# A third attention batch on the TensorE-transposed path, a split first token group, and masking by matmul in a fused attention and SiLU-MLP kernel

## The chip, the cores and the metric

The kernel runs on one core of a Trainium2 chip. The metric is the device time of one execution in microseconds (us), as a median of several executions. A single-core program has no second die to compare with; runs are called fast unless they lie more than 1.5% above the fastest of their kernel, and only fast runs are compared. The time of an execution is about 1.7 us longer than the span of its profile (before: 341.09 against 339.4).

## The reference

Windowed attention over 8 batches, 8 heads, 576 positions and 64 features; heads 0 to 3 see a plain window of the last 32 positions, heads 4 to 7 a dilated one (every fourth of the last 128). The result, 4608 tokens of 512 features, goes through a two-layer MLP.

```python
scores = scale * np.matmul(q, k.transpose(0, 1, 3, 2))
mask_plain = (rel >= 0) & (rel < 32)
mask_dil   = (rel >= 0) & (rel < 32 * 4) & (rel % 4 == 0)
scores = np.where(masks, scores, -1e9)              # heads 0-3 plain, 4-7 dilated
attn = softmax(scores)                              # q, k, v: (8, 8, 576, 64) float32
x = (attn @ v).transpose(0, 2, 1, 3).reshape(4608, 512)
h = x @ w_in                                        # (512, 2048)
out = (h * sigmoid(h)) @ w_out                      # (2048, 512)
```

## The kernel before

The Python code does not only emit instructions, it plans them: a small simulator with assumed durations and assumed DMA arrival times decides in which order the steps are put into each engine's queue. The order is then fixed, and each engine works through its queue in that order. Every number below that looks like a time in the code is such an assumption.

q and k must be transposed before the scores. There are two ways in the kernel:

- **TensorE path** (batches 0 and 1, `PEB = 2`): q and k are loaded to SBUF as fp16 (`nat`), transposed by TensorE against an identity (`td`, `ta`, `tb`), and the attention result is transposed back by TensorE (`xp`, `xd`) into `xA`.
- **DMA path** (all other batches): a GpSimd DMA casts q and k to an fp16 scratch in DRAM (`kq_s`), DMA transposes on the SP queue bring them in (`nat<-kq_s`, `kqT<-kq_s`; four of them make a "turn"), and the attention result goes out to `x_s` and comes back by another DMA transpose (`xA<-x_s`, `xR<-x_s`).

The MLP runs in groups of 512 tokens. Layer 1 of a group needs x of all its tokens, so it needs one or two batches of attention.

```python
GT = 512;  NG = NT // GT            # 9 groups
PEB = 2;  GA = 3;  XR = 4           # batches on the TensorE path; groups in xA; buffers xR
# ... (cut)
issue_nat(0)                        # q, k of batch 0, all heads
# ... identity, band masks (cut)
issue_v(0)
# ... (cut)
for f0 in range(0, DFF, FC):        # w_in, 4 DMAs
    nc.gpsimd.dma_start(out=w_in16[:, :, f0 : f0 + FC], in_=wi[:, :, f0 : f0 + FC])
issue_nat(1)
for f0 in range(0, NFF, 4):         # w_out, 4 DMAs
    nc.gpsimd.dma_start(out=w_out16[:, f0 : f0 + 4], in_=wo[:, f0 : f0 + 4])
issue_v(1)
# ... (cut)
def turn_gen(b):
    issue_turn(b)                   # four DMA transposes on the SP queue
    yield "DMA", 12.5
    if b + 1 < B:
        count(("L", b + 1), loads_need(b + 1), lambda: start_loads(b + 1))

def loads_gen(b):
    # fences on the turn of batch b-1 and on x of batch b-2 (cut)
    issue_v(b)
    issue_cast(b)                   # q, k to the fp16 scratch
    yield "DMA", max(9.0, 52.0 - plan.now)
    v_in[b].done = plan.now
    yield "DMA", 4.5
    count(("T", b), 2, lambda: start_turn(b))
# ... in scores(): (cut)
nc.tensor.matmul(sp[i][:, w*n : w*(n+1)], lhs, rhs, start=True, stop=True)
nc.scalar.activation(p2, both[:, :, :n], AF.Exp, scale=scale)
nc.vector.tensor_tensor(p2, p2, mk, ALU.mult)        # the mask
# ... layer 1, one step of 16 per group: (cut)
for c in range(HP):
    nc.tensor.matmul(h, w_in16[:, c, f*P : (f+1)*P], x_g[:, c], start=(c == 0), stop=(c == HP-1))
nc.scalar.activation(th, h, AF.Tanh, scale=0.5)
nc.vector.scalar_tensor_tensor(gTs[g][:, f], th, 1.0, h, ALU.add, ALU.mult)
```

The softmax here doesn't subtract the row's maximum and nothing guards it: scores larger than these inputs give would overflow.

## Time and profile before

| | before |
|---|---|
| time, median | 337.68 us (337.23 to 342.65, 3 runs) |
| profiled run | 341.09 us, so 3.4 us above the median |
| first layer-1 matmul | 28.80 us |
| TensorE busy | 304.1 us of 339.4 |

The page of the kernel before. PE is TensorE, DVE is VectorE, ACT is ScalarE. The rows of digits give the busy tenths in 40 equal slices of the span (8.5 us each); PEclk is the clock granted to TensorE, in tenths.

```profile
span 339.4 us, 5670 instructions
...
PE 304.1 (90%) x2200; PEld 147.2 (43%) x2200; DVE 200.3 (59%) x477; ACT 154.2 (45%) x258; POOL 49.5 (15%) x78
...
PE   0678998999999883999999999599999999999995
...
PEclk9999999999999997999999999879999999999999
...
```

TensorE is close to full except at the start, in slices 14 to 16 and slice 26. The timeline of TensorE at the start of the kernel before (start, length, line, operation, output and inputs, shape, count, and in brackets the idle time before it and its releaser):

```profile
...
10.76 1.04 PE L404 MATMUL td<-ident,nat 96*128 96x96 f16 x11 [3.87 <-DMA nat<-in_q_dram]
...
28.80 4.93 PE L636 MATMUL h<-xA,w_in 128*128 128x512 f16 x12
34.10 2.07 PE L636 MATMUL h<-xA,w_in 128*128 128x512 f16 x8 [0.36 <-DVE gT L647]
...
```

The first transposes wait for data until 10.76 us; layer 1 begins at 28.80, and its first 12 matmuls take 4.93 us where eight take 2.07 later: the clock is still low. (The row PEclk shows 9 there all the same. The trace has no clock record before 32.93 us, and the page counts time without a record as full clock; in the first slices the matmul durations have to be read instead.) The waits of TensorE from 60 us on (total, times, longest):

```profile
...
PE h L636 <- DMA xR<-x_s: 6.0, 1, 6.0
PE s L434 <- DMA nat<-kq_s: 3.6, 1, 3.6
...
```

Two waits for DMA stand out: 6.0 us for the transposed x of batch 3 (it ends at 132.5 us) and 3.6 us for the transposed k and q of batch 7. The SP queue ahead of the first:

```profile
...
115.03 6.91 SPq L131 DMA_TRANSPOSE nat<-kq_s  x2
122.04 2.72 SPq L135 DMA_TRANSPOSE kqT<-kq_s  x2
124.85 0.85 SPq L507 DMA_DIRECT2D x_s<-oD  x1
127.77 2.53 SPq L326 DMA_TRANSPOSE xR<-x_s  x1
```

The last store of batch 3 (`x_s<-oD`) stands in the queue behind the turn of batch 4, and the transpose back to `xR` follows it.

### The profile page before, as it was taken

To read this page: it belongs to the slowest core of one execution; us is meant where nothing else is said; L and a number is where in the kernel's file an instruction comes from. 1 tells how busy PE (TensorE), PEld (TensorE's weight loads), DVE (VectorE), ACT (ScalarE), POOL (GpSimd) and SP (SyncE) were. 2 spreads that over 40 slices of the span, in tenths; PEclk is the share of its full clock that TensorE was granted. 3 is DMA by queue.
4 is the path that set the end of the run, shared out by engine and by line. 5 is a ranking of instruction groups with operands and counts; after the bars stand their busy time and mean duration, and the time that the engine had idled before them with its cause. 6 is when DMAs were issued, how large, how long until landed. Compare 5 with 4: busy or idle time off the path is not lost.

```text
span 339.4 us, 5670 instructions
## 1 busy us (share of the span) xinstructions
PE 304.1 (90%) x2200; PEld 147.2 (43%) x2200; DVE 200.3 (59%) x477; ACT 154.2 (45%) x258; POOL 49.5 (15%) x78
## 2 busy tenths in 40 slices
PE   0678998999999883999999999599999999999995
PEld 0553544444444331445444344244444444444442
DVE  5684779859977641698776368477654254145100
ACT  1464664156545440666455366254454344244211
POOL 8823410140005003100320050000000000000000
PEclk9999999999999997999999999879999999999999
DMA  8999999899759995995699989972260100200121
GB/s 104 187 206 199 204 174 214 180 165 214 163 150 147 205 214 80 192 231 143 150 188 228 212 106 202 221 138 77 79 144 33 62 31 0 95 1 31 64 93 62
DMA packets 115899, 47.42 MB, mean 140 GB/s; under 512 B 82592, under 2 KB 111264, under 8 KB 115872
## 3 DMA queue, kind: packets, MB, share of 16 engines
q0 software_dynamic: 47152, 19.92, 47.5%
q1 hardware_dynamic: 63536, 17.70, 26.6%
q10 hardware_dynamic: 5184, 9.44, 8.1%
q8 instruction: 17, 0.28, 0.3%
q14 instruction: 10, 0.08, 0.1%
HBM read 39.84 MB, written 20.05 MB: 176 GB/s over the span
## 4 chain that ended last, share of the span: by engine, by line
PE 80%; DVE 7%; DMA 6%; ACT 4%; issue 1%; POOL 1%; ACTq 0%; SPq 0%; POOLq 0%
PE y L664 36%; PE h L636 35%; PE s L434 3%; PE av_d L470 2%; DMA nat<-in_q_dram 2%; DVE gT L647 2%; PE av_p L470 2%; ACT th L645 2%; ACT ob L675 1%; DMA xR<-x_s 1%; DMA nat<-kq_s 1%; DVE oD L474 1%; DVE oP L474 1%; PE td L404 1%; DVE probs L449 1%
## 5 line engine op out<-in xcount | busy, mean ns | idle before, releaser
L647 DVE SCALAR_TENSOR_TENSOR gT<-th,h 128x512 f16<-128x512 f32 x144 | 98.0, 684 | 79.9 <-ACT th L645 79.7
L664 PE MATMUL y<-w_out,gT 128*128 128x512 f16 x576 | 140.3, 381 | 2.4 <-ACT ob L675 1.9
L645 ACT ACTIVATE th<-h 128x512 f32<-128x512 f32 x144 | 86.1, 598 | 93.3 <-PE h L636 89.0
L636 PE MATMUL h<-xR,w_in 128*128 128x512 f16 x384 | 95.7, 388 | 6.1 <-DMA xR<-x_s 6.0
L636 PEld LDWEIGHTS <-w_in 128*128 128x128 f16 x576 | 54.8, 100 | 73.7 <-issue 12.0
L664 PEld LDWEIGHTS <-gT 128*128 128x128 f16 x576 | 53.2, 98 | 60.8 <-issue 3.0
L636 PE MATMUL h<-xA,w_in 128*128 128x512 f16 x192 | 48.5, 390 | 2.8 <-DVE gT L647 2.6
L442 ACT ACTIVATE probs<-s 128x768 f16<-128x768 f32 (+2 forms) x45 | 36.4, 810 | 22.3 <-PE s L434 19.8
L675 ACT ACTIVATE ob<-y 128x512 f32<-128x512 f32 x36 | 21.5, 597 | 50.1 <-PE y L664 49.9
L470 PEld LDWEIGHTS <-probs 128*128 128x128 f16 x448 | 23.5, 102 | 15.5 <-issue 1.9
L474 DVE TENSOR_TENSOR oD<-av_d,rcps 72x256 f16<-72x256 f32 x64 | 26.9, 421 | 2.2
L474 DVE TENSOR_TENSOR oP<-av_p,rcps 96x256 f16<-96x256 f32 x48 | 20.2, 421 | 1.6
L449 DVE TENSOR_TENSOR probs<-probs,mask_d 128x864 f16<-128x864 f16 (+1 forms) x24 | 13.2, 552 | 6.8 <-ACT probs L442 6.6
L310 POOL COPY fence<-kqT 128x1 f16<-128x1 f16 x10 | 2.4, 240 | 99.7 <-DMA kqT<-kq_s 99.7
L470 PE MATMUL av_d<-vd,probs 128*128 128x65 f16 x256 | 15.9, 201 | 1.0 <-DVE rcps L473 0.6
L449 DVE TENSOR_TENSOR probs<-probs,mask_p 128x768 f16<-128x768 f16 x24 | 13.3, 553 | 6.0 <-ACT probs L442 5.7
L473 DVE RECIPROCAL rcps<-av_d 72x4 f32<-72x4 f32 x64 | 11.0, 172 | 7.6 <-PE av_d L470 7.5
L470 PE MATMUL av_p<-vp,probs 128*128 128x65 f16 x192 | 13.4, 200 | 1.5 <-DVE probs L449 0.9
L404 PE MATMUL td<-ident,nat 96*128 96x96 f16 x48 | 4.3, 242 | 10.5 <-DMA nat<-in_k_dram 6.6
L155 POOL DMA_DIRECT2D vp<-in_v_dram x8 | 11.6, 1446 | 3.5 <-PE td L404 1.9
L141 POOL DMA_DIRECT2D vraw<-in_v_dram x16 | 10.8, 677 | 5.1 <-DMA nat<-in_k_dram 2.4
L473 DVE RECIPROCAL rcps<-av_p 96x4 f32<-96x4 f32 x48 | 8.3, 174 | 4.3 <-PE av_p L470 3.6
(62 smaller groups left out, 117.0 us busy)
## 6 DMA issues: line engine op xcount, KB each, us to landing
out_dram<-ob ACTq DMA_DIRECT2D x36, 256.0 KB, 2.1
kq_s<-in_k_dram POOLq DMA_DIRECT2D x6, 576.0 KB, 9.8
kq_s<-in_q_dram POOLq DMA_DIRECT2D x6, 576.0 KB, 12.5
vp<-in_v_dram POOLq DMA_DIRECT2D x7, 384.0 KB, 7.5
w_in<-in_moe_w_in_dram POOLq DMA_DIRECT2D x4, 512.0 KB, 11.9
w_out<-in_moe_w_out_dram POOLq DMA_DIRECT2D x4, 512.0 KB, 16.6
vraw<-in_v_dram POOLq DMA_DIRECT2D x8, 224.0 KB, 5.6
x_s<-oP SPq DMA_DIRECT2D x12, 144.0 KB, 2.6
```

The lines of the kernel that those rows point to most:

```text
L141: nc.gpsimd.dma_start(out=vraw[p0 : p0 + m1 - m0, ab].rearrange("p h r d -> p h (r d)"), in_=src[m0:m1],)
L155: nc.gpsimd.dma_start(out=vp[:, j0:, :D], in_=win)
L442: nc.scalar.activation(p2, both[:, :, :n], AF.Exp, scale=scale)
L449: nc.vector.tensor_tensor(p2, p2, mk, ALU.mult)
L470: nc.tensor.matmul(a[:, i, : D + 1], lhs(i), rhs(i), start=True, stop=True)
L473: nc.vector.reciprocal(rcp[:n], a[:n, :, D : D + 1])
L474: nc.vector.tensor_tensor(o, a[:n, :, :D], rcp[:n, :, None].broadcast_to([n, HN, D]), ALU.mult)
L636: nc.tensor.matmul(h, w_in16[:, c, f * P : (f + 1) * P], x_g[:, c], start=(c == 0), stop=(c == HP - 1),)
L645: nc.scalar.activation(th, h, AF.Tanh, scale=0.5)
L647: nc.vector.scalar_tensor_tensor(gTs[g][:, f], th, 1.0, h, ALU.add, ALU.mult)
L664: nc.tensor.matmul(y, gTs[g][:, f, tb * P : (tb + 1) * P], w_out16[:, f], start=(f == 0), stop=(f == NFF - 1),)
L675: nc.scalar.activation(ob, y, AF.Copy, scale=0.5)
```

## The change

Its intent: TensorE waits for the DMA path, so one more batch is kept off it (`PEB = 3`), and the start is shortened: the dilated half of batch 0 is loaded and attended first; the first 512 tokens become two groups of 256, so that layer 1 can begin after half of batch 0; the masks of batch 0 are added in PSUM, where the results of matmuls collect, by a matmul (identity times 0 or -32768) instead of being multiplied on VectorE; layer 1 of the first two groups may use five PSUM buffers. Layer 2's weights are loaded before batch 1, and a turn is issued in four parts, so that stores can slip between its transposes.

```diff
-    NG = NT // GT
+    GROUPS = [(0, GT // 2), (GT // 2, GT // 2)] + [(t, GT) for t in range(GT, NT, GT)]
+    NG = len(GROUPS)
-    PEB = 2
-    GA = 3
-    XR = 4
+    PEB = 3
+    GA = 4
+    XR = 3
+    BIG = 32768.0
+    BIASED = (0,)
@@ start (cut) @@
-    issue_nat(0)
+    issue_nat(0, HN, H)              # dilated heads first
     make_identity(nc, ident)
-    issue_v(0)
+    issue_vraw(0)
+    issue_nat(0, 0, HN)              # then the plain heads
+    issue_vp(0)
+    nc.vector.tensor_scalar(band, band, 1.0, BIG, ALU.subtract, ALU.mult)
     # w_in
-    issue_nat(1)
     # w_out
-    issue_v(1)
+    issue_nat(1, 0, H)
+    issue_vraw(1)
+    issue_vp(1)
+    def third_batch():
+        issue_nat(2, 0, H)
+        issue_vraw(2)
+        issue_vp(2)
+        issue_cast(PEB)
+        yield "DMA", 0.0
@@ turns (cut) @@
-        issue_turn(b)
-        yield "DMA", 12.5
+        for n, us in enumerate((3.0, 3.0, 1.5, 7.5)):
+            issue_turn(b, n)
+            yield "DMA", us
@@ scores (cut) @@
+            if biased:
+                for i in range(2):
+                    nc.tensor.matmul(sp[i][:, : w * len(blocks)], ident, bs, start=True, stop=False)
@@
-                        sp[i][:, w * n : w * (n + 1)], lhs, rhs, start=True, stop=True
+                        sp[i][:, w * n : w * (n + 1)], lhs, rhs, start=not biased,
+                        stop=not biased or n == len(blocks) - 1,
@@
+            if biased:
+                return
             nc.vector.tensor_tensor(p2, p2, mk, ALU.mult)
@@ layer 1 (cut) @@
-            Step(lambda ring, f=f: l1(f), 0.87, ["h"], list(deps) + [AT_WIN[f // 4]], ("ACT", "DVE"))
+            Step(
+                lambda ring, f=f: l1(ring, f), 0.01 + w / 595, ["h", "x"] if g < 2 else ["h"],
+                list(deps) + [AT_WIN[f // 4]], ("ACT", "DVE"),
+            )
```

Cut from the diff: new orders of the attention steps, copies that go to whichever of ACT and DVE the planner finds free, seven score sets instead of six on the TensorE path, and new assumed arrival times.

## The prediction

> **What bounds the kernel now.** TensorE: busy 304 of 339.4 us (page, part 1), 80% of the chain that ended last. Adding each matmul at its warm interval (four 128x512 in 0.86 us in the timeline; small ones about 32 ns) gives an estimated 287 us of work. The other 52 us, by PE's timeline, the waits and the table of stretches:
> 1. Start: first matmul at 6.6 us, q of batch 0 lands at 10.6, layer 1 begins at 28.8 with 7.9 us of warm work done: 21 us lost. Batch 0's attention is one chain of short PE, ACT and DVE steps.
> 2. Layer 1 alone, 29 to 37: 1.2 us a step instead of 0.86, through two PSUM buffers, tanh (0.60) and multiply (0.69). With the cold clock, 4 us.
> 3. 126.5 to 132.5: layer 1 waits 6.0 us for batch 3's transposed x (xR<-x_s). In the SP queue batch 3's last store stands behind batch 4's transposes, which wait for a cast. Granted clock then 0.83 over 10 us: 8 us in all.
> 4. 214.8 to 218.4: scores of batch 7 wait 3.6 us for nat<-kq_s, then clock 0.86 and 0.80: 7 us.
> 5. 4 us after the last matmul; small waits.
> The Trainium skill, "TensorE: Matmul & The Clock Gate", Part 1, says an idle TensorE falls to half clock until busy about 3.4 us; the granted clock agrees (0.83 after the 6.0 us wait).
>
> **What the change does.**
> - PE gains 14 bias matmuls (4608 columns, 1.9 us warm, twice that cold) and a third batch's transposes (3.1): by the instruction orders 292 us, +5.3.
> - Start: dilated half of k and q first, so transposes start near 8.4 instead of 10.7; seven mask multiplies (0.45 to 0.6 us each, two in the chain) go. Layer 1 begins on 256 tokens after three of six plain blocks and half the dilated ones: first matmul at 21 to 23 with 8.0 done. Loss 14, gain 7.
> - Layer 1 of two half groups over five buffers: gain about 2.
> - Layer 2's weights before batch 1: layer 2 starts near 43, batch 1's data arrive then, and its attention (29 us long in the old timeline, 37 to 66) must fit beside 14 us of layer 2: 2 to 4 us of new waits around 45 to 65.
> - One batch fewer on the DMA path, its first cast early, its transposes split in four so stores slip between: the chain load, cast, transpose, attention, store, transpose leads TensorE by an estimated 15 us. Stalls 3 and 4 mostly go: gain 10 to 15.
>
> **Sum.** 339.4 + 5 - 7 - 2 + 3 - 13, some eaten by small waits of the planned in-order queue: 319 to 325 on the profile's scale, the timed median about 1 lower. I predict 321 us, 80% range 313 to 330. Faster by over 2%: 0.87; within 2%: 0.10; slower: 0.03.
>
> **What would show it.** First h matmul near 22 us (wrong after 25). No wait above 2 us on xR, xA<-x_s or nat<-kq_s after 100 us, clock 1.0 in every slice from there. PE waits of a few us on DVE and ACT between 45 and 65. No mask multiplies on DVE in batch 0; bias matmuls near 0.24 us cold.
>
> **What would make it wrong.** The DMA stalls stay or move (batch 4's cast waits for batch 2's readers); the PE order, fixed from assumed arrivals, meets later data (w_out near 28 to 36, batch 1 near 42), each miss idling PE and costing a warm-up; half-size matmuls hide weight loads less well (98 against 107 ns).

## The result, and the profile after

| | before | after |
|---|---|---|
| time, median | 337.88 us (337.23 to 342.65, 4 runs) | 328.11 us (327.89 to 328.73, 4 runs) |
| ratio of fast runs | | 0.972 (95%: 0.9697 to 0.9743) |
| span of the profile | 339.4 us | 327.0 us |
| first layer-1 matmul | 28.80 us | 24.93 us |

A ratio is the mean time of one kernel's fast runs over the mean of the other's fast runs of the same rounds, so it is not quite the ratio of the medians in the table. The change makes the kernel 2.8% faster; I had forecast 321 us, and it takes 328. The profiles differ by 12.4 us, the medians by 9.8, because the profiled run before was a slow one of its kind.

The page after:

```profile
span 327.0 us, 6033 instructions
...
PE 306.0 (94%) x2354; PEld 156.4 (48%) x2354; DVE 203.3 (62%) x501; ACT 160.8 (49%) x296; POOL 52.9 (16%) x83
...
PE   0798999898999999999999999899999999999995
...
PEclk9999999989999999999999999999999999999999
...
```

The low slices in the middle are gone. TensorE at the start of the changed kernel:

```profile
...
8.43 2.00 PE L465 MATMUL td<-ident,nat 96*128 96x96 f16 x23 [2.93 <-DMA nat<-in_q_dram]
...
15.44 0.50 PE L440 MATMUL ta<-ident,pair_rest 96*128 96x96 f16 x4 [0.79 <-DVE pair_rest L523]
...
24.93 0.60 PE L717 MATMUL h<-xA,w_in 128*128 128x256 f16 x4
...
29.24 3.23 PE L717 MATMUL h<-xA,w_in 128*128 128x256 f16 x28
...
44.92 0.93 PE L465 MATMUL td<-ident,nat 96*128 96x96 f16 x18
...
66.30 1.91 PE L717 MATMUL h<-xA,w_in 128*128 128x512 f16 x4
...
```

The dilated transposes start at 8.43, as forecast. The plain ones cannot finish before 15.44, and layer 1 begins at 24.93, two to four us later than forecast. Then 28 half-size matmuls take 3.23 us with their drain: the weight loads stay hidden behind the smaller matmuls. Batch 1 starts at 44.92, when its data land. At 66.30 four matmuls of the next group need 1.91 us instead of about 1.03: TensorE had been waiting on the end of batch 1's attention, and the clock had dropped (granted clock 0.83 between 60 and 70 us). The chain that ended last names what 15.44 waits for, the plain half of q:

```profile
...
5.42 1.31 POOL vraw L146 x2
6.72 1.88 POOL nat L116 x3
8.61 6.32 DMA nat<-in_q_dram
15.44 1.15 PE ta L440 x12
...
```

It lands at 14.93 us, behind v; before, all of batch 0 was in by 10.6. The waits of TensorE from 60 us on, and the SP queue around the first transpose back:

```profile
...
PE s L500 <- DMA nat<-kq_s: 1.2, 1, 1.2
...
```

```profile
...
100.99 2.85 SPq L137 DMA_TRANSPOSE nat<-kq_s  x1
...
115.18 0.84 SPq L580 DMA_DIRECT2D x_s<-oD  x1
117.98 1.38 SPq L369 DMA_TRANSPOSE xA<-x_s  x1
```

No DMA wait above 1.2 us is left. The turn of batch 4 starts at 100.99 us, against 115.03 before. x of the first batch on the DMA path is being transposed at 117.98 us, and TensorE reaches the group that needs it at 124.33.

**Where the time went.** To compare kernels whose queues are ordered differently, I use "lost time": the start of the first layer-1 matmul of a group, minus the estimated warm duration of all matmuls ahead of it in TensorE's queue. The durations are intervals read from the timelines: 0.216 us for 512 columns (four in 0.86), 0.110 for 256, 0.043 for 96, 0.033 for 65 or 72. The position in the trace is found by counting; the counts of trace and instruction list agree to within 4 records, so the values hold to about half a microsecond, but beside a wait a miscount of one matmul is worth the whole wait. Token 1536 of the kernel before and of b_turn4 is such a place, and there the first matmul that reads xR is taken from the trace:

```profile
...
132.49 3.28 PE L636 MATMUL h<-xR,w_in 128*128 128x512 f16 x8 [5.97 <-DMA xR<-x_s]
...
```

The sum of all work by the same estimate is 286.9 us before and 292.2 after.

| lost time (us) at the group that begins at token | 0 | 512 | 1024 | 1536 | 2048 | 3072 | 4096 |
|---|---|---|---|---|---|---|---|
| before | 21.8 | 28.3 | 30.2 | 38.8 | 40.7 | 48.3 | 48.0 |
| after | 17.0 | 21.9 | 26.7 | 27.1 | 27.8 | 30.5 | 30.9 |

After the last group only full-speed MLP work and a tail of 4 us follow. Up to token 512 the change gains 6.4 us; it gives back 2.9 of them by token 1024; from 1024 to the end it gains another 13.6; and it adds 5.3 us of work. That makes 11.8 of the 12.4 us. But a table of gains in order of time does not say which part of the change caused them: for that, parts were taken out.

### The profile page after: what moved, and what is told of

Read it like the earlier page. It is cut to its first block, busy times and chain, and to the rows that moved or that the text cites. A ratio compares the mean times of both kernels' runs of the same rounds, so it can differ in the third digit from the quotient of the medians.

```text
span 327.0 us, 6033 instructions
## 1 busy us (share of the span) xinstructions
PE 306.0 (94%) x2354; PEld 156.4 (48%) x2354; DVE 203.3 (62%) x501; ACT 160.8 (49%) x296; POOL 52.9 (16%) x83
## 4 chain that ended last, share of the span: by engine, by line
PE 80%; DVE 9%; DMA 4%; ACT 3%; POOL 2%; issue 1%; ACTq 0%; SPq 0%; POOLq 0%
PE y L750 36%; PE h L717 34%; PE s L500 3%; DVE gT L728 3%; DVE oD L549 2%; DMA nat<-in_q_dram 2%; DMA nat<-kq_s 2%; PE av_d L545 2%; PE av_p L545 2%; POOL nat L116 1%; DVE oP L549 1%; ACT ob L761 1%; DVE rcps L548 1%; PE td L465 1%; PE ta L440 1%
## 5 line engine op out<-in xcount | busy, mean ns | idle before, releaser
L750 PE MATMUL y<-w_out,gT 128*128 128x512 f16 x576 | 138.7, 379 | 0.9 <-ACT ob L761 0.9
L728 DVE SCALAR_TENSOR_TENSOR gT<-th,h 128x512 f16<-128x512 f32 (+1 forms) x160 | 99.6, 630 | 58.7 <-ACT th L726 57.7
L726 ACT ACTIVATE th<-h 128x512 f32<-128x512 f32 (+1 forms) x160 | 88.8, 556 | 77.4 <-PE h L717 71.0
L717 PEld LDWEIGHTS <-w_in 128*128 128x128 f16 x640 | 59.5, 98 | 55.2 <-issue 4.1
L717 PE MATMUL h<-xR,w_in 128*128 128x512 f16 x320 | 76.5, 379 | 0.5 <-DVE gT L728 0.4
L717 PE MATMUL h<-xA,w_in 128*128 128x512 f16 (+1 forms) x320 | 63.5, 339 | 1.3 <-DVE oD L549 0.7
L509 ACT ACTIVATE probs<-s 128x768 f16<-128x768 f32 (+2 forms) x45 | 35.0, 777 | 28.7 <-PE s L500 24.8
L761 ACT ACTIVATE ob<-y 128x512 f32<-128x512 f32 x36 | 21.5, 598 | 45.0 <-PE y L750 44.9
L545 PEld LDWEIGHTS <-probs 128*128 128x128 f16 x448 | 22.5, 99 | 12.6 <-DVE probs L518 0.4
L549 DVE TENSOR_TENSOR oD<-av_d,rcps 72x256 f16<-72x256 f32 x64 | 26.9, 421 | 2.2
L549 DVE TENSOR_TENSOR oP<-av_p,rcps 96x256 f16<-96x256 f32 x48 | 20.2, 421 | 1.6
L518 DVE TENSOR_TENSOR probs<-probs,mask_p 128x768 f16<-128x768 f16 x21 | 11.6, 554 | 8.8 <-ACT probs L509 8.8
L518 DVE TENSOR_TENSOR probs<-probs,mask_d 128x576 f16<-128x576 f16 (+1 forms) x23 | 11.9, 517 | 2.9 <-ACT probs L509 2.6
L465 PE MATMUL td<-ident,nat 96*128 96x96 f16 x72 | 5.7, 249 | 8.2 <-DMA nat<-in_k_dram 5.2
L163 POOL DMA_DIRECT2D vp<-in_v_dram x8 | 11.7, 1466 | 8.9 <-PE av_p L545 6.2
## 6 DMA issues: line engine op xcount, KB each, us to landing
w_in<-in_moe_w_in_dram POOLq DMA_DIRECT2D x4, 512.0 KB, 11.4
w_out<-in_moe_w_out_dram POOLq DMA_DIRECT2D x4, 512.0 KB, 17.9
```

The costliest lines, as they stand in the source:

```text
L163: nc.gpsimd.dma_start(out=vp[:, j0:, :D], in_=win)
L545: nc.tensor.matmul(a[:, i, : D + 1], lhs(i), rhs(i), start=True, stop=True)
L549: nc.vector.tensor_tensor(o, a[:n, :, :D], rcp[:n, :, None].broadcast_to([n, HN, D]), ALU.mult)
L717: nc.tensor.matmul(h[:, :w], w_in16[:, c, f * P : (f + 1) * P], x_g[:, c], start=(c == 0), stop=(c == HP - 1),)
L726: nc.scalar.activation(th[:, :w], h[:, :w], AF.Tanh, scale=0.5)
L728: nc.vector.scalar_tensor_tensor(gTs[g][:, f, :w], th[:, :w], 1.0, h[:, :w], ALU.add, ALU.mult)
```

## The experiments

Twelve kernels in three lots of four. The four of a lot ran on the same chip and share their runs of the kernel before, which took 338.69, 340.91 and 338.51 us (median) in the three lots; the lots are rows 1 to 4, 5 to 8 and 9 to 12 of the table. Neither times nor ratios compare freely across lots. In each lot the kernel before has executions below 339.1 us and others above 340. In the second lot five of those above 340 count as fast, in the other two none does, so the mean of its fast runs is 338.0, 340.3 and 336.9 us, and that alone makes the ratios of the second lot 0.7 to 1% lower than those of the others. The second and third lots ran on the same chip, so there a time can also be set beside that of the control after_again, 327.62 us. All gave a correct result.

| kernel | median us | ratio to before (95%) | first layer-1 matmul |
|---|---|---|---|
| a_nobias | 327.21 | 0.9685 (0.9659 to 0.9711) | 26.57 |
| a_nosplit | 327.06 | 0.9685 (0.9656 to 0.9715) | 29.20 |
| a_peb2 | 338.17 | 1.0018 (0.9982 to 1.0053) | 24.15 |
| b_turn4 | 337.05 | 0.9955 (0.9917 to 0.9993) | 29.07 |
| c_third | 330.20 | 0.9691 (0.9641 to 0.9740) | 28.59 |
| a_both | 328.83 | 0.9661 (0.9612 to 0.9710) | 30.20 |
| a_warm | 327.57 | 0.9615 (0.9567 to 0.9664) | 24.81 |
| a_b1first | 328.35 | 0.9629 (0.9572 to 0.9686) | 24.57 |
| after_again | 327.62 | 0.9736 (0.9694 to 0.9778) | 25.83 |
| a_peb2_cast1 | 370.00 | 1.0921 (1.0825 to 1.1017) | 25.23 |
| a_best | 321.63 | 0.9559 (0.9521 to 0.9597) | 24.57 |
| a_best2 | 373.04 | 1.1041 (1.0967 to 1.1116) | 21.07 |

The lost times:

| lost time (us) at token | 0 | 512 | 1024 | 1536 | 2048 | 3072 | 4096 |
|---|---|---|---|---|---|---|---|
| a_peb2 | 16.2 | 20.5 | 27.3 | 36.8 | 41.9 | 43.4 | 43.1 |
| b_turn4 | 21.2 | 29.5 | 32.4 | 42.3 | 45.2 | 47.3 | 47.1 |
| a_nosplit | 20.2 | 25.2 | 26.7 | 26.8 | 27.2 | 28.9 | 29.1 |
| c_third | 21.5 | 30.1 | 30.6 | 31.1 | 31.6 | 32.2 | 31.9 |
| a_both | 23.2 | 26.9 | 29.3 | 30.0 | 31.0 | 31.9 | 31.8 |
| a_b1first | 16.6 | 22.5 | 23.7 | 24.4 | 24.8 | 30.7 | 30.1 |
| a_best | 16.6 | 20.2 | 20.4 | 21.1 | 22.2 | 23.1 | 23.0 |

### a_nobias: masks multiplied again

```diff
-    BIASED = (0,)
+    BIASED = ()
-    nc.vector.tensor_scalar(band, band, 1.0, BIG, ALU.subtract, ALU.mult)
-    nc.vector.memset(mask_p[:W, :2], -BIG)
+    nc.vector.memset(mask_p[:W, :2], 0.0)
```

> The changed kernel with the bias matmuls of batch 0 taken out and the seven mask multiplies on DVE put back (everything else kept, the planner re-plans the order). Theory A (the start is limited by TensorE itself at the cold clock, and the 14 bias matmuls are 3 to 4 us of it between 10 and 24 us): first layer-1 matmul 2 to 3 us earlier than 24.9, time 325 to 327 us against 328.1. Rival (the reason for the change: two multiplies and their hops leave the chain): first layer-1 matmul about 1 us later, time 329 to 330.

Measured: first layer-1 matmul at 26.57 us, 1.6 us later than in the changed kernel, and 327.21 us, ratio 0.9685. Each theory got one half wrong. Theory A's early start did not come: TensorE loses the bias matmuls but waits for the multiplies instead. The rival's later start came, but not its longer time. The bias matmul does shorten the start, by 1.6 us against the changed kernel's profile and by 0.7 against the control's (25.83), and nothing of it reaches the end.

### a_nosplit: one first group of 512 tokens

```diff
-    GROUPS = [(0, GT // 2), (GT // 2, GT // 2)] + [(t, GT) for t in range(GT, NT, GT)]
+    GROUPS = [(t, GT) for t in range(0, NT, GT)]
```

> The changed kernel with the first 512 tokens as one group again. Theory A: layer 1 can then begin only after the whole of batch 0, first matmul 28 to 29 us instead of 24.9, though the attention before it no longer shares TensorE with layer 1: time 330 to 332 against 328.1. Rival (the chain to the end of batch 0 is what counts, and the early half only fills gaps that layer 2 or later steps would give back): within 1 us of 328.1.

Measured: the start was as theory A said, 29.20 us; the time was as the rival said, 327.06 us. In the table of lost times a_nosplit is 3.3 us behind the changed kernel at token 512 and level with it at token 1024 (26.7 both). Whatever layer 1 gains by beginning 4.3 us earlier is gone 30 us later.

### a_peb2: the third batch taken out

```diff
-    PEB = 3
-    GA = 4
-    XR = 3
+    PEB = 2
+    GA = 3
+    XR = 4
     def third_batch():
-        issue_nat(2, 0, H)
-        issue_vraw(2)
-        issue_vp(2)
         issue_cast(PEB)
```

(One more wait in the planner's list lets the first cast be issued before its turn, and the assumed arrival of that cast is 55 us instead of 64.)

> The changed kernel with two batches on the TensorE-transposed path again, the start and the four-part turns kept. Theory A (the third batch gives the DMA path its lead, and without it waits of 3 us or more on xR or nat<-kq_s come back after 90 us): time 331 to 335. Rival B (the four-part turns alone cured the DMA waits, and the third batch only adds 3.1 us of transposes to TensorE): 324 to 326 with no wait above 2 us.

Measured: 338.17 us, ratio 1.0018: all of the gain is gone, more than theory A had said. This kernel starts layer 1 at 24.15 us and is 7.8 us ahead of the kernel before at token 512 (20.5 lost against 28.3). Of that lead 2.9 us are left at token 1024 and 2.0 at token 1536 (36.8 against 38.8), and at token 2048 it is 1.2 us behind. Its waits from 60 us on:

```profile
...
PE h L715 <- DVE gT L726: 4.9, 9, 1.6
PE h L715 <- DMA xR<-x_s: 4.5, 1, 4.5
...
```

The wait for xR is back, and its transpose was issued at 128.26 us, against 127.77 before. The DMA path runs at its own pace (the turn of batch 4 starts at 117.4 us, against 115.0 before), and TensorE, arriving early, only waits more: first in layer-1 steps for VectorE, then for the DMA itself. That those steps wait because few layer-2 steps run beside them is my reading, not shown. (At token 4096 this profile has lost 4.9 us less than that of the kernel before, for 2.3 us more of work, and its span is 2.8 us shorter. The profiled run before was a slow one of its kind; the medians of the lot, 338.17 and 338.69, are the comparison.)

### b_turn4: the kernel before with the turn in four parts

```diff
-        issue_turn(b)
-        yield "DMA", 12.5
+        for n, us in enumerate((3.0, 3.0, 1.5, 7.5)):
+            issue_turn(b, n)
+            yield "DMA", us
```

> The kernel before with one edit: the four transposes of a turn are issued at four times of the plan, so the stores of the batch before slip between them in the SP queue. Theory B (the 6.0 us wait for x of batch 3 came from the order of the SP queue): that wait goes, time 330 to 333 against 337.9. Rival A (the chain of load, cast, transpose, attention, store is too long for its lead whatever the queue's order): the waits stay or move, 336 to 339.

Measured: 337.05 us, ratio 0.9955; the record's verdict is "unclear". Theory B falls: it was my reading of the SP queue in the prediction. Stores now do stand between the transposes, and the wait has moved:

```profile
...
PE h L637 <- DMA xR<-x_s: 3.6, 1, 3.6
...
```

```profile
...
122.40 3.10 SPq L132 DMA_TRANSPOSE nat<-kq_s  x1
...
136.05 2.20 SPq L327 DMA_TRANSPOSE xR<-x_s  x1
...
```

The turn of batch 4 is now at 122.40 instead of 115.03, and the transpose to xR at 136.05 instead of 127.77. Letting one transfer pass another did not shorten the chain. (This profile, of 340.2 us, and that of the kernel before are both of slower executions; of the faster ones there is no profile.)

### c_third: the third batch nearly alone

The edits of a_nobias and a_nosplit, and the loads as in the kernel before: batch 0 whole, batch 1's k and q before w_out. The new orders and the turns in four parts stay.

> The third batch nearly alone: the changed kernel with one first group of 512 tokens, mask multiplies instead of bias matmuls, batch 0 loaded whole and batch 1's k and q loaded before layer 2's weights, as in the kernel before. Theory C (the third batch is the whole gain; the early start is given back by 100 us): time 326 to 329 against 337.9 for before and about 328 for the changed kernel. Rival (the gain needs both, the start and the third batch): 331 to 334.

Measured: ratio 0.9691, with layer 1 starting at 28.59 as before the change; the median of 330.20 us goes with 340.91 for the kernel before in this lot. Theory C holds in the main. By the ratio the gain is whole without the early start; by the time it is 2.6 us short of the control on the same chip (330.20 against 327.62), which leaves 8.3 of the 10.9 us that the control gains on the kernel before in its lot. So the third batch carries three quarters of the gain or more. (c_third keeps the new orders and the four-part turns; whether the third batch needs them was not tested. Without the third batch, in a_peb2, they gain nothing.) The lost time at token 512 (30.1) is even larger than before (28.3), and from there to the end only 1.8 us are added, against 19.7 before.

What the third batch does can be read from the SP queues. The turn of batch 4 in c_third:

```profile
...
99.31 3.33 SPq L137 DMA_TRANSPOSE nat<-kq_s  x1
...
```

The turns of batches 3, 4, 5, 6 and 7 start at 79.0, 115.0, 145.5, 180.0 and 210.3 us before; at 65.3, 101.0, 135.1, 168.3 and 202.2 after; and at 61.7, 99.3, 129.7, 162.2 and 193.8 in c_third. Without the third batch, in a_peb2, they are at 82.8, 117.4, 148.5, 183.5 and 214.3. The first batch that goes through the scratch is then batch 3; its cast is issued at 49.7 us instead of 69.9, and the path keeps that lead of 8 to 18 us to the end.

### a_both: bias and split both undone

> The changed kernel with both the bias matmuls and the split of the first group undone. Alone each measured 0.9685 of before against 0.972 for the changed kernel. Theory C (neither matters to the end, each costs about 1 us of extra TensorE work): 325.5 to 327.5. Rival (one of the two is needed to keep the start short): 329 to 331.

Measured: ratio 0.9661, 328.83 us where before takes 340.91. By the ratio theory C holds again (0.9661 of 337.9 us is 326.4); by the time it lies between the two theories, 1.2 us above the control. The difference to c_third is only the order of the loads: a_both has lost less at token 512 (26.9 against 30.1) and loses 4.9 us from there to the end, where c_third, with batch 1 before layer 2's weights, loses 1.8.

### a_warm: dummy matmuls before the first data

```diff
+    nc.vector.memset(xA[:, 0, :512], 1.0)
+    hot = ps_s.tile([P, 2, 512], F32, tag="s", name="hot")
+    for _ in range(16):
+        nc.tensor.matmul(hot[:, 0], xA[:, 0, :P], xA[:, 0, :512], start=True, stop=True)
     issue_nat(0, HN, H)
```

> The changed kernel with 16 dummy matmuls of 512 columns on a constant tile before the data arrive, to have TensorE's clock granted before 8.4 us. The result is not touched. Theory C (batch 1's k and q land near 45 us, and its attention ends near 65 whatever the start does): first layer-1 matmul moves from 24.9 to 21 to 23 us, and the time stays within 1 us of 328. Rival A (the start counts in full): 324 to 326.

Measured: first layer-1 matmul at 24.81 us, not 21 to 23; 327.57 us. The dummies brought the clock up, and it was lost again. Stretches of 2 us (length, then busy us and instructions of each engine, granted clock, DMA share, GB/s):

```profile
...
8.00:10.00 2.00, 2.00 (x33) 1.43 (x31) 1.98 (x8) 0.00 (x0) 2.00 (x4) 1.00 1.15 144
10.00:12.00 2.00, 1.58 (x29) 0.92 (x25) 1.14 (x4) 1.23 (x3) 1.96 (x2) 1.00 1.17 147
12.00:14.00 2.00, 0.80 (x12) 0.49 (x9) 1.35 (x4) 0.06 (x1) 1.36 (x2) 0.79 1.40 169
14.00:16.00 2.00, 0.40 (x6) 0.30 (x5) 0.77 (x2) 0.00 (x0) 1.77 (x4) 0.50 2.16 147
16.00:18.00 2.00, 2.00 (x28) 1.91 (x26) 1.19 (x5) 1.59 (x5) 1.43 (x2) 0.50 1.65 189
...
```

In the gap before the plain half of q (landing about 15 us) the granted clock fell to 0.5 and stayed there until 23.4 us. The experiment therefore does not say what a warm start is worth: it shows that arrival of data, not the clock, made the gap. (a_best2, below, says more.) The ratio of 0.9615 is lower than those of its neighbours, in part because of its lot; the time is that of the control, 327.62 us, and I make nothing of it.

### a_b1first: batch 1 loaded before layer 2's weights

```diff
+    issue_nat(1, 0, H)
+    issue_vraw(1)
+    issue_vp(1)
     for f0 in range(0, NFF, 4):
         nc.gpsimd.dma_start(out=w_out16[:, f0 : f0 + 4], in_=wo[:, f0 : f0 + 4])
-    issue_nat(1, 0, H)
-    issue_vraw(1)
-    issue_vp(1)
```

(The planner's arrival times for batch 1 and w_out are changed to match.)

> The changed kernel with batch 1's k, q and v loaded before layer 2's weights, and the planner's arrival times changed to match. Theory C (after the early start TensorE waits for batch 1's attention around 62 to 66 us, and loses 5 us between tokens 512 and 1024): batch 1's attention starts near 33 to 35 instead of 45, the loss goes, time 323 to 326. Rival (VectorE, over 90% busy from 80 to 110 us, sets that stretch): within 1 us of 328.

Measured: 328.35 us with a wide spread (325.83 to 331.35), ratio 0.9629. In the stretch it was made for, theory C holds: batch 1's first transpose runs at 34.98 us instead of 44.92, and between tokens 512 and 1024 the kernel loses 1.2 us instead of 4.8; at token 2048 it is 3.0 us ahead of the changed kernel. Then 5.9 us are lost between tokens 2048 and 3072, most of them after a wait of 2.8 us near 203 us:

```profile
...
203.19 2.69 PE L717 MATMUL h<-xR,w_in 128*128 128x512 f16 x8 [2.80 <-DVE gT L728]
...
```

ScalarE stood for 3.4 us at that point, by the table of waits for a DMA of the SP queue (`x_s<-oP`) whose data it does not use (a_peb2_cast1, below, shows how that comes about). So the time of this kernel alone decides neither way.

### after_again: the changed kernel as a control

> The changed kernel itself, as a control on the same chip as the three runs with it. Expected: 0.972 of before, about 328 us where before takes 338.

Measured: 327.62 us, ratio 0.9736. As expected; so the last lot compares with 327.62 us.

### a_peb2_cast1: another way to give the DMA path a lead

On a_peb2: the scratch casts of the first two DMA batches are issued together, and each later one a batch early.

```diff
         issue_cast(PEB)
+        issue_cast(PEB + 1)
@@ in loads_gen @@
-        if b > PEB:
-            issue_cast(b)
+        if PEB < b < B - 1:
+            issue_cast(b + 1)
+        if b > PEB:
+            count(("T", b), 2, lambda: start_turn(b))
         yield "DMA", 9.0
         v_in[b].done = plan.now
-        if b > PEB:
-            yield "DMA", 4.5
-            count(("T", b), 2, lambda: start_turn(b))
```

> The changed kernel with two batches on the TensorE path (which alone fell back to 338 us), but with each batch's cast of k and q to the scratch issued one batch earlier, so that its transposes need not wait for the cast. Theory D (what the third batch buys is lead of the DMA path, 13 us or so; any other lead does as well, and saves its 3.1 us of transposes): x of batch 3 is there 10 us or more before 128, time 325 to 330. Rival (the third batch helps by taking attention work off the DMA path and its queues; the cast was hidden already): 334 to 339.

Measured: 370.00 us. Neither theory foresaw it. Its profiled run took 372.56 us and counts as slow (the six runs spread from 364.52 to 374.33), so the following describes this kernel and explains no small difference. The turns of batches 2 and 3 now run back to back from 54 to 84 us, at the same time as the loads of v and the next casts. The DMAs of the whole run (size, median us from issue to landing), first of a_peb2_cast1, then of a_peb2:

```profile
...
kq_s<-in_k_dram POOLq DMA_DIRECT2D x6, 576.0 KB, 18.2
...
vp<-in_v_dram POOLq DMA_DIRECT2D x7, 384.0 KB, 16.6
...
nat<-kq_s SPq DMA_TRANSPOSE x12, 12.7
...
```

```profile
...
kq_s<-in_k_dram POOLq DMA_DIRECT2D x6, 576.0 KB, 9.3
...
vp<-in_v_dram POOLq DMA_DIRECT2D x7, 384.0 KB, 7.3
...
nat<-kq_s SPq DMA_TRANSPOSE x12, 5.6
...
```

These three kinds take about twice as long; the loads of w_in (11.7 against 11.4 us) do not. The Trainium skill, "DMA: Bandwidth & Descriptors", section "Issuing engines are not separate DMA queues", says that DMAs started by different engines run on the same 16 DMA engines and interleave; this trace agrees. And one wait was not of data at all:

```profile
...
ACT probs L507 <- DMA kqT<-kq_s: 12.8, 1, 12.8
ACT probs L507 <- PE s L498: 4.8, 2, 4.3
...
```

ScalarE stands 12.8 us for a transpose whose result it does not read, and TensorE 11.4 us for ScalarE. By the semaphore numbers in the trace, the DMAs of the SP and ACT queues share eight completion counters (111 to 118). The store of the output just ahead in ScalarE's queue waits on counter 113 until 70.01 us, and the last user of that counter was the transpose `kqT<-kq_s` issued at 65.99. In a_b1first it is counter 111, which `x_s<-oP` had used last. So the test of theory D is void: the lead was bought with contention and with a blocked ScalarE. Whether a lead got in another way would do what the third batch does is left open.

### a_best: batch 1 early, the plain half early, dummies

The edits of a_b1first and a_warm, and:

```diff
-    issue_vraw(0)
     issue_nat(0, 0, HN)
+    issue_vraw(0)
     issue_vp(0)
```

> The changed kernel with batch 1's data before layer 2's weights, the plain half of batch 0 issued before v, and 16 dummy matmuls before the first data. Theory C (arrival of data sets the start: plain half at 14.9 us in the changed kernel, batch 1 at 45): plain half lands near 12 to 13, first layer-1 matmul near 20 to 22, loss at token 1024 2 to 4 us smaller than in the changed kernel; time 1 to 1.5% below the control, about 324. Rival (the start is given back wherever it is gained): within 0.4% of the control.

Measured: 321.63 us (321.32 to 322.41), ratio 0.9559, against 0.9736 for the control on the same chip: 1.8% faster than the changed kernel (0.9559 / 0.9736 = 0.982) and 4.4% faster than the kernel before. The total gain is a little more than the 1 to 1.5% of theory C; the way to it is only in part as it said:

```profile
...
13.74 0.50 PE L444 MATMUL ta<-ident,pair_rest 96*128 96x96 f16 x4 [1.93 <-DVE pair_rest L527]
...
24.57 0.60 PE L721 MATMUL h<-xA,w_in 128*128 128x256 f16 x4
...
```

```profile
...
35.76 0.68 PE L469 MATMUL td<-ident,nat 96*128 96x96 f16 x12
...
```

The plain transposes finish their wait at 13.74 instead of 15.44, but the first layer-1 matmul, expected at 20 to 22 us, stays at 24.57. Batch 1 begins at 35.76 instead of 44.92. Lost time is 3.6 us between tokens 0 and 512 and 0.2 between 512 and 1024 (the changed kernel: 4.9 and 4.8), and no single wait after 60 us is above 0.4 us. Which share of the step from a_b1first to a_best belongs to the earlier plain half, to the dummies, or to a planned order that happens to avoid the late wait, was not separated.

### a_best2: the same with two batches and early casts

> Both of the two before: two batches on the TensorE path, casts one batch earlier, batch 1's data before layer 2's weights, plain half before v, dummy matmuls. If theories C and D both hold: the lowest of all, 321 to 325. If D fails: 333 to 338, like the kernel with two batches.

Measured: 373.04 us: it has the fault of a_peb2_cast1 (ScalarE stands once for 12.8 us, and the median landing time of the k casts is 20.5 us), and of the total it says no more than that one. Its start, though, answers in part what a_warm left open:

```profile
...
13.02 0.34 PE L442 MATMUL ta<-ident,pair_rest 96*128 96x96 f16 x4 [0.73 <-DVE pair_rest L525]
...
21.07 0.60 PE L719 MATMUL h<-xA,w_in 128*128 128x256 f16 x4
...
```

Up to the first layer-1 matmul its TensorE queue is that of a_best. There the granted clock fell to 0.5 at 13.35 us, the same four transposes took 0.50 us from 13.74, and layer 1 began at 24.57. Here the clock stayed at 1.00 until 35 us, and layer 1 began at 21.07. The transposes start 0.7 us earlier here, so from this one pair of profiles I estimate the kept clock at about 2.8 us of the start.

## Why the prediction was right or wrong

**Right: faster, inside the range, and the DMA waits after 100 us go.** The forecast was 313 to 330 us, the result 328.11. No wait above 1.2 us on xR, xA or the transposed k and q remains, and the granted clock is full in every slice from 100 us on, as stated.

**Right: the bound.** TensorE bounds the kernel; its work rose by an estimated 5.3 us and the time still fell. The half-size matmuls did not expose their weight loads (28 in 3.23 us with their drain).

**Wrong: the size.** 321 us forecast, 328 measured, a gain of 9.8 us instead of 17. The first cause is bookkeeping: the sum in the prediction, 339.4 + 5 - 7 - 2 + 3 - 13, is 325.4, and I shaded it to 321 without a reason; moreover it starts from a profiled run that was itself 3.4 us above its median, and then takes away the waits of that run in full. Without the shading the sum was only 1.6 us from the 327.0 measured on the profile's scale, and the table of lost times has terms near the predicted ones (6.4 gained at the start, 2.9 given back, 13.6 gained later). That agreement is partly luck: the next point shows that the start's term does not reach the end.

**Wrong: the step "Start ... first matmul at 21 to 23 with 8.0 done. Loss 14, gain 7".** The first matmul came at 24.93 and the gain there was 4.8 us of lost time (21.8 to 17.0). I had taken the changed kernel's own assumed arrival of the plain half (12.8 us); it landed at 14.93. That is the smaller part: in a_best the plain half is 1.7 us earlier and the first matmul still comes at 24.57, and only in a_best2, where the granted clock stays at 1.00, does it come at 21.07. The larger fault is that I added this gain to the total at all. a_peb2 keeps the whole early start and measures 1.0018; c_third drops it and measures 0.9691, or 2.6 us more than the control; a_nobias and a_nosplit each undo one piece of it and lose nothing. The term that should have been 7 was between 0 and 2.6.

**Wrong: the step "2 to 4 us of new waits around 45 to 65".** The place was right, the size was not: from token 256 to token 1024 the lost time grows by 8.0 us (18.7 to 26.7). Batch 1's data land near 45 us because layer 2's weights were put before them, its attention ends near 65, and a TensorE that started early has by then nothing else to do. a_b1first (up to token 2048) and a_best move that arrival and keep the gain. This is what ate the start.

**Wrong: the cause given for the wait of 6.0 us.** I blamed the order of the SP queue. b_turn4 changes that order alone, and what it gains is unclear: about 0.5% (0.1 to 0.8), with a wait of 3.6 us left. What helped was the third batch: turns 8 to 14 us earlier than before. That the third batch causes most of the gain is shown by taking it out and by having it nearly alone; that it does so through the lead of the DMA path rests on those turn times, and the attempt to give the lead by other means failed for reasons of its own.

**About right: "gain 10 to 15" from the DMA waits.** In the changed kernel the lost time after token 1024 falls from 17.8 us to 4.2, a gain of 13.6. With the third batch nearly alone it falls by 17.9 us after token 512 (19.7 to 1.8); the 3.1 us of added transposes are counted apart, as in the sum.

## What to carry to other kernels

Savings at different places of a timeline add up only if nothing between them is tied to absolute time: here a start 4 us earlier ran into data that still landed at 45 us, and earlier work on two batches ran into a DMA chain that still delivered at 128. Before crediting an earlier start, follow the queue forward to the next arrival that the start does not move, and move that first. When a change has several parts, take each out and also run each alone: here the third batch carried three quarters of the gain or more, and moving loads, with a few dummy matmuls, gained another 1.8%.

## What the Trainium skill lacked or had wrong

- "TensorE: Matmul & The Clock Gate", Part 1, has the clock fall back after at least one idle window of about 3.4 us. A later section of Part 1, on a second failure mode, says that frequent short idle times can do it too; neither says how much activity counts as busy. Here no idle stretch of 3.4 us was needed. In the 3.41 us before the granted clock fell to 0.5, TensorE was busy for 2.22 us in a_warm (9.77 to 13.18), 1.55 in a_best (9.94 to 13.35) and 2.05 in the changed kernel (61.70 to 65.11); after 2.42 busy of 3.41 us in a_best2 (11.16 to 14.57) it did not fall. The page's half rate agrees with the changed kernel (1.91 us for four matmuls at 66.30 us, 1.03 when warm).
- "DMA: Bandwidth & Descriptors" says that queues share the 16 DMA engines, but gives no figure for DMA transposes beside casting loads. In a_peb2_cast1 against a_peb2 the median landing time of the transposes of k and q rose from 5.6 to 12.7 us, that of the v loads from 7.3 to 16.6 us.
- No page says that DMAs issued by two engines can take their completion counters from one shared set, so that a store holds its engine until another engine's transfer has landed. In a_peb2_cast1 this held ScalarE for 12.8 us, in a_b1first for 3.4 us.
